# Attention beside a long convolution on one core: when products with V may wait, when the output weights are loaded, and the convolution's allowance

## The chip, the core and the metric

The kernel runs on one core of a Trainium2 chip. The core has a matrix engine (TensorE, PE in the profile; its weight loads are listed as PEld), a vector engine (VectorE, DVE), an engine for functions such as exponentials and sines (ScalarE, ACT), GpSimd (POOL) and SyncE (SP), which here only issues DMAs. Each engine works through its own instructions in order. The metric is device time in microseconds (us), the median of several runs; lower is better.

## What is computed

Two independent parts, concatenated along the last axis. All inputs are fp32.

```
part A (state space convolution), L = 2048, D = 576, N = 128
  dt = exp(log_dt);  A = A_re + i A_im;  B, C complex
  K[d, l] = Re sum_n C[d,n] * exp(dt[d] A[d,n] l) * dt[d] B[d,n]
  y = causal convolution of u with K along l  (reference: FFT of length 2L)
  a = y + u * Dskip

part B (attention, 32 query heads of width 18, one shared key/value head), S = 2048
  q = x wq (32 heads);  k = x wk;  v = x wv
  p = softmax(q k^T / sqrt(18));  o = p v;  b = o wo

result = concat(a, b)          # 2048 x 1152
```

## The kernel before

**The attention** is the spine of the program. Queries are taken in four chunks c of 512 rows, heads in pairs, keys in 16 blocks kb of 128. A *tile* is one pair of heads against one block of keys: `scores` (L466) computes it on PE into one of NS = 3 PSUM buffers "s", `exponentials` (L474) turns it into probabilities "P" on ACT (NP = 8 buffers), and `product` (L765) multiplies two tiles, which is four heads, with V on PE into "ops". So there are 2048 heads-times-blocks in 1024 tiles and 512 products. A *round* handles three tiles: their scores, their exponentials, and the one or two products that come due; `self.step` counts products, so one round is 1.5 steps, and there are 342 rounds. Sixteen steps are a *group* of four heads; `fetch` (L455) then brings the query operands "aug" of later pairs from a DRAM buffer "qd" with SyncE. `gather` copies a finished group out of PSUM ("o") and stores it ("od").

**The side work** of the attention is projections: `qproj` makes the queries of 128 columns at a time ("q", L344) and `queries` stores them to "qd" with GpSimd; `outproj` and `outproj_part` multiply normalised outputs with the output weights "wo_sb" ("op"). The last chunk's remaining output products, and its normalisation, are done after the loop in `finish` ("fin").

**The convolution** works on 12 blocks k of 48 channels. `front(k)` makes the kernel K from small tables of sines, cosines and exponentials: `arguments` and `factors` on DVE and ACT, `tables` ("tab") on DVE, `kgen` ("kg") on PE. Odd blocks prepare the factors of the next even block too (tile "stage") and store them ("fr"). `back(k)` transforms u and K ("hu", "lu", "hk", "lk"), multiplies the spectra on DVE ("us", "ks", "acc", "pt"), and transforms back ("iy"); "outa" is stored at its end. ACT needs another table for sines than for exponentials, so the sines of a block are issued together, as a *burst*: a table load, two or four sines (L1048, L1049), and a table load back before the next exponential of the attention (L474).

**What sets the order.** The instruction order on PE, ACT and DVE is written out when the program is built, by a planner. `Clock` holds estimated times: K.t of PE, K.a of ACT, K.v of DVE, K.s the times at which the three score buffers come free. In each round of `main`, after scores and exponentials, `fill(then)` puts side work and convolution work on PE until the estimated time `then`, each product is placed, and `free()` says when the next scores can begin. A product may stay behind for one round:

```
while behind < r // 2:
    fill(free() - 0.88 * (r // 2 - behind))
    if behind == r // 2 - 1 and K.t + 0.88 > free() + DEFER:
        break
    product(behind)
    behind += 1
```

The side work and the convolution are generators that say at each yield what they need next: "p" a piece of PE work, "v" a piece of DVE work, "w" wait, "b" a burst of sines. A "b" is held until 8 or more pieces of projection work are open (`beside`), or 16 steps have passed. The convolution has a budget: `Conv.go` refuses work when what it has placed on DVE is over 20 us above `step * RATE`, and lets DVE's queue run deeper (up to 1 us) by how far it is below `step * RATE`. `Conv.lags` is true when it is below `step * PACE` and has a piece of PE work next; side work is then passed over, unless a due time is within 8 steps or a projection is half done.

**Loads.** `load_wo` (L326 and L328) writes one element per row block of wo_sb with DVE and then issues five DMAs on SyncE; because of the memset, they wait for DVE to reach it. It is called as the first thing of `main`. `Conv.start` (the transform matrices "dft", L1292, and two blocks of u, L969) stands just ahead of it on SyncE, the first `fetch` of queries just behind.

Of the kernel before, what the change touches and what calls it, by code (L numbers as in the profile page):

```python
# [38 lines left out]
NP = 8  # L39


RATE = 1.79
PACE = 1.72
AHEAD = 0.7
TOTAL = 340.0
LAST = 500
DEFER = 0.5
# [134 lines left out]
class Attention:  # L182
# [521 lines left out]
    def main(self, conv, flag):  # L704
        nc, K = self.nc, self.k
        conv.beside = lambda: self.o_left + self.q_left
        side = self.side_work
        self.load_wo()
        K.t = K.v = K.a = self.o_free = 0.0
        K.fill = 0.0  # L710
        side.ready = 0.0
        for st in conv.streams:
            st.ready = 0.0
        prep = Stream(self.prepare(), K, 99.0)
        pairs = [(c, g, kb, j) for c in range(NCH) for g in range(8) for kb in range(16) for j in range(2)]
        state = dict(credit=0.0, filled=0.0)

        def holder():
            return next((st for st in [side] + conv.streams if st.holds), None)

        def force(done):
            while not done():
                st = holder()
                (side if st is None else st).advance()
                self.fetch(self.group)

        def fill(then):

            t, idle = K.t, 0.0
            more = True  # L730
            while more:
                more = False
                credit = state["credit"] - (K.t - t - idle)
                urgent = self.due < self.step + 8
                late = self.late()
                for st in (prep, side, conv) if urgent else (prep, conv, side):

                    if st is side and side.kind == "p" and not (urgent or side.holds) and conv.lags(self.step):
                        continue
                    spare = credit - 0.3 if st is not side or urgent or late or side.holds else 0.0  # L740
                    wait = then - K.t - (1.2 if st is side and not urgent and not side.holds and self.units > 0.6 * self.step + HEAD else 0.15)
                    if st.go(self.step, max(spare, wait, 0.3 * (st is side and side.holds and conv.lags(self.step) and credit > -1.0)), holder()):
                        more = True
                        break
                else:

                    at = min((x for x in (st.event() for st in [prep, side] + conv.streams) if x > K.t), default=then)
                    if at < then - 0.5:
                        idle += at - K.t
                        K.t = at  # L750
                        more = True
            t += idle
            if K.t > t:
                K.t += 0.03
            state["filled"] += K.t - t
            state["credit"] = max(state["credit"] - (K.t - t), -0.8)

        def product(n):
            nonlocal o_ps
            c, g, kb, _ = pairs[2 * n]  # L760
            if kb == 0:
                fill(self.o_free)
                o_ps = self.ps_o.tile([P, CT], F32, tag="o", name=f"ops{c}_{g}")
            for j in range(4):
                nc.tensor.matmul(o_ps[32 * j:32 * j + 32, :], self.v[:, kb, :], pts[2 * n + j // 2][:, j % 2, :],  # L765
                                 start=(kb == 0), stop=(kb == 15), tile_position=(0, 32 * j))
            K.pe(0.88, done[2 * n + 1] + 0.1, self.o_free if kb == 0 else 0.0)
            read[n] = K.t + 0.2
            state["credit"] -= 0.88
            if kb == 15 and (c, g) != (NCH - 1, 7):  # L770
                self.gather(c, g, o_ps)
                if g == 7:
                    self.todo.append((c, range(5)))
                if c == NCH - 1 and g in LATE:
                    self.todo.append((c, LATE[g]))
        o_ps, pts, done, read, behind = None, {}, {}, {}, 0
        for r in range(0, len(pairs), NS):
            new = range(r, min(r + NS, len(pairs)))
            self.step = new[-1] // 2
            ss = {}  # L780
            for i in new:
                c, g, kb, j = pairs[i]
                if (g, kb, j) == (0, 0, 0):
                    self.od[c] = self.dr.tile([8 * P, CT], F32, tag="od", name=f"od{c}")
                force(lambda: 16 * c + 2 * g + j in self.ready)
                ss[i] = self.scores(i, c, 2 * g + j, kb, 0.335 if i == r else 0.215)
            K.t += 0.22
            for i in new:

                while (i - NP) // 2 >= behind:  # L790
                    product(behind)
                    behind += 1
                c, g, kb, j = pairs[i]
                pts[i] = self.exponentials(i, c, 2 * g + j, kb, *ss[i], read.get((i - NP) // 2, 0.0))
                done[i] = K.a
            s = self.step

            state["credit"] = min(state["credit"] + NS / 2 * (0.88 + min(max((TOTAL - state["filled"]) / max(LAST - s, 20), 0.45), 0.7 if s < 384 else 0.9)), 1.2 + 0.88)

            def free():  # L800

                return max(K.s[(r + NS + j) % NS] - 0.22 * j for j in range(NS))
            while behind < r // 2:
                fill(free() - 0.88 * (r // 2 - behind))

                if behind == r // 2 - 1 and K.t + 0.88 > free() + DEFER:
                    break
                product(behind)
                behind += 1
            fill(free())  # L810
            c, g, kb, j = pairs[new[-1]]
            self.group = (new[-1] + 1) // 32
            self.fetch(self.group)
            nxt = 16 * c + 2 * g + 3
            if kb >= 12 and nxt < 64:
                force(lambda: nxt in self.ready)
        while behind < len(pairs) // 2:
            product(behind)
            behind += 1

        while self.todo or self.busy or holder() or any(m == 0 for _, _, m in self.rest):
            if self.todo or self.busy:
                prep.advance()
            elif holder() or self.outs:
                (holder() or side).advance()
        conv.drain()
        nc.vector.tensor_scalar(flag, self.ubound[0:1, :], LIMIT / (2 * SCALE), None, op0=ALU.is_le)
        self.finish(NCH - 1, self.part, o_ps, self.w4, self.b4)
# [86 lines left out]
class Conv:  # L915
# [100 lines left out]
    def factors(self, k):  # L1016


        nc, V, p1, K = self.nc, self.V, self.pf, self.k
# [5 lines left out]
        if k % 2 == 0 and k > 0:  # L1025
            yield "v", self.kept_ready, False
            f, r = self.kept
        else:
            f, r, m = (p1.tile(shp, F32, tag=t, name=f"{n}{k}") for t, n in (("f", "f"), ("r", "r"), ("sum", "m")))
# [13 lines left out]
            if both:  # L1043
                nc.scalar.activation(m2, m2, AF.Exp)
                K.act(1.25)
            yield "b", K.v + 0.3, False
            for r_, f_ in ((r, f), (r2, f2)) if both else ((r, f),):
                nc.scalar.activation(r_, r_, AF.Sin, scale=-TWO_PI, bias=self.hp)  # L1048
# [229 lines left out]
    def early(self):  # L1278
        nc = self.nc
        nc.scalar.dma_start(self.pos, self.a["pos"])  # L1280
        self.load(0)
        self.n = -1
        self.streams = [Stream(self.front(0), self.k)]

    def begin(self):
# [19 lines left out]
    def go(self, step, credit, lock):  # L1305
        self.turn()
        lag = step * RATE - self.work
        if lag < -20.0:
# [16 lines left out]
    def lags(self, step):  # L1325
        return self.work < step * PACE and any(st.live and st.kind == "p" for st in self.streams)

# [105 lines left out]
```

## Time and profile before

| what | value |
|---|---|
| median of 3 runs (lowest to highest) | 1222.99 us (1221.77 to 1226.05) |
| the profiled execution, and its span | 1222.96 us, 1221.1 us |
| mean clock granted to PE | 0.985 |
| PE, ACT, DVE, POOL busy | 94%, 85%, 80%, 10% |
| bytes moved by DMA, mean rate | 102.15 MB, 84 GB/s |
| exponentials of the attention on ACT | 1024 of 1030 ns, 968.6 us |
| matmul instructions of the products with V, of the scores | 4096 (520.9 us busy), 2048 (366.3 us busy) |

How to read it. The page of the profile lists the busy time of each engine, the chain of work that ended last (each step followed back to what released it), and groups of instructions by line, `out<-in` in the program's names, count and duration. A row in order of time has start, length, engine, line, operation, operands, the count of instructions merged, and in brackets the idle time of the engine ahead of it with what ended it. A row of windows has a stretch of time, its length, each engine's busy time with its instruction count, PE's granted clock (1.00 is full), the mean busy share of the 16 DMA engines, and GB/s. Rows with SPq or ACTq are the queues that issue. An fp32 matmul of the program shows as two instructions, so a product is 8 rows' worth and a score tile 2. "issue" means that nothing visible was late.

### The profile page before, as it was taken

Reading aid. Unit: us, or ns where it says so; the run is one execution under the profiler, and the core shown is the slowest. Engines: PE = TensorE matmul, PEld = TensorE weight load, DVE = VectorE, ACT = ScalarE, POOL = GpSimd, SP = SyncE. Lnnn points to the kernel's source line nnn. Section 1 sums busy time; section 2 is a strip of 40 time slices with the busy share of each in tenths; the row PEclk is TensorE's granted clock in tenths of the full one; section 3 lists DMA queues with packets and bytes.
Section 4 is the critical chain, followed back from the end, with each engine's and each line's share of the span. In section 5 each row is a group of like instructions: output and inputs, shape, how many; then the busy total and the mean of one; then the engine's idle time right before and its main releaser. Section 6 shows DMA issues by size and latency. Waiting matters only on the chain.

```text
span 1221.1 us, 32917 instructions
## 1 busy us (share of the span) xinstructions
PE 1141.8 (94%) x13852; PEld 471.5 (39%) x13852; DVE 973.2 (80%) x1599; ACT 1033.3 (85%) x1091; POOL 118.6 (10%) x210
## 2 busy tenths in 40 slices
PE   5989899999899999989999989999997999989997
PEld 1433333434343444434344334444342434433433
DVE  4757965997997896996997996993975899689684
ACT  2769989878898988998898998888899888899891
POOL 2220401011211000011020000002040000000000
PEclk9989999999999999999999999999998999999999
DMA  7533323124243112132234122114123111211201
GB/s 227 146 131 88 103 81 114 39 60 120 87 143 98 60 35 86 40 126 92 69 103 138 41 69 91 50 56 115 61 75 119 69 51 35 90 45 43 67 28 55
DMA packets 61713, 102.15 MB, mean 84 GB/s; under 512 B 17692, under 2 KB 28570, under 8 KB 61048
## 3 DMA queue, kind: packets, MB, share of 16 engines
q1 hardware_dynamic: 47046, 85.32, 21.4%
q0 software_dynamic: 13824, 14.07, 4.4%
q8 instruction: 111, 1.82, 0.6%
q10 hardware_dynamic: 690, 0.60, 0.2%
q14 instruction: 42, 0.34, 0.1%
HBM read 55.66 MB, written 42.89 MB: 81 GB/s over the span
## 4 chain that ended last, share of the span: by engine, by line
PE 70%; DVE 12%; ACT 10%; issue 4%; DMA 4%; SPq 1%; ACTq 0%; DVEq 0%
PE ops L765 29%; PE s L466 21%; ACT P L474 8%; PE q L344 4%; PE op L179 4%; PE iy L179 3%; PE kg L1130 3%; DVE ks L109 2%; DMA xr<-xT 2%; PE hu L179 1%; DVE acc L109 1%; PE fin L179 1%; DVE tab L109 1%; PE hk L179 1%; DVE pt L109 1%
## 5 line engine op out<-in xcount | busy, mean ns | idle before, releaser
L474 ACT ACTIVATE P<-s 128x1024 f32<-128x1024 f32 x1024 | 968.6, 1030 | 144.5 <-PE s L466 142.3
L765 PE MATMUL ops<-P,v_sb 128*32 128x512 f32 x4096 | 520.9, 602 | 14.0 <-DVE o L113 13.9
L466 PE MATMUL s<-aug,kaug 55*128 55x512 f32 x2048 | 366.3, 445 | 35.0 <-ACT P L474 27.7
L466 PEld LDWEIGHTS s<-aug,kaug 55*128 55x128 f32 x2048 | 170.1, 186 | 348.8 <-ACT P L474 311.9
L765 PEld LDWEIGHTS ops<-P,v_sb 128*32 128x32 f32 x4096 | 114.2, 110 | 163.5 <-issue 118.5
L409 POOL DMA_DIRECT2D qd<-qh x116 | 66.0, 575 | 466.9 <-DVE qh L113 466.8
L344 PE MATMUL q<-x,wq_sb 128*32 128x256 f32 x1360 | 85.3, 385 | 1.1 <-DVE un L121 1.0
L179 PE MATMUL op<-wo_sb,oT 126*32 126x288 f32 (+1 forms) x1040 | 74.1, 409 | 4.0 <-DVE ob L113 2.7
L113 DVE COPY ksb<-kg 128x192 f32<-128x192 f32 x48 | 17.4, 364 | 58.0 <-PE kg L1130 57.7
L109 DVE TENSOR_TENSOR tab<-tab,tt 128x576 f32<-128x576 f32 (+1 forms) x72 | 59.1, 821 | 1.8
L109 DVE TENSOR_TENSOR tab<-r,dif 128x576 f32<-128x576 f32 (+1 forms) x72 | 58.8, 816 | 0.0
L109 DVE TENSOR_TENSOR tab<-sum,r 128x576 f32<-128x576 f32 (+1 forms) x72 | 58.7, 816 | 0.0
L109 DVE TENSOR_TENSOR tab<-tab 128x576 f32<-128x576 f32 (+1 forms) x72 | 58.7, 815 | 0.0
L109 DVE TENSOR_TENSOR tt<-f,sum 128x576 f32<-128x576 f32 (+1 forms) x72 | 58.6, 815 | 0.0
L344 PEld LDWEIGHTS q<-x,wq_sb 128*32 128x32 f32 x1360 | 40.8, 111 | 45.4 <-issue 20.4
L109 DVE TENSOR_TENSOR acc<-acc,pt 128x1728 f32<-128x1728 f32 (+2 forms) x36 | 48.6, 1350 | 0.3
L109 DVE TENSOR_TENSOR pt<-us,ks 128x1728 f32<-128x1728 f32 (+2 forms) x36 | 48.1, 1350 | 0.1
L179 PEld LDWEIGHTS op<-wo_sb,oT 126*32 126x32 f32 (+1 forms) x1040 | 30.4, 109 | 44.3 <-issue 17.6
L109 DVE TENSOR_TENSOR u<-u,iy 128x384 f32<-128x384 f32 x24 | 13.3, 553 | 39.1 <-PE iy L179 39.0
L1130 PEld LDWEIGHTS kg<-tab 128*32 128x32 f32 x2304 | 36.2, 110 | 21.2 <-issue 12.0
L446 POOL DMA_DIRECT2D qd<-sh x19 | 12.0, 633 | 315.2 <-DVE sh L117 311.3
L1130 PE MATMUL kg<-tab 128*32 128x64 f32 x2304 | 41.7, 220 | 0.0
(134 smaller groups left out, 999.3 us busy)
## 6 DMA issues: line engine op xcount, KB each, us to landing
aug<-qd SPq DMA_DIRECT2D x124, 110.0 KB
od<-o SPq DMA_DIRECT2D x31, 256.0 KB
fr<-stage SPq DMA_DIRECT2D x10, 624.0 KB
qd<-qh POOLq DMA_DIRECT2D x24, 216.0 KB, 4.6
u<-u SPq DMA_DIRECT2D x12, 384.0 KB
kd<-ksb SPq DMA_DIRECT2D x12, 384.0 KB
kt<-kd SPq DMA_DIRECT2D x48, 96.0 KB
outa<-u SPq DMA_DIRECT2D x12, 384.0 KB
```

Of the source, the lines that this page charges most:

```text
L109: return self.v.tensor_tensor(out, *a, **k)
L113: return self.v.tensor_copy(out, *a, **k)
L179: nc.tensor.matmul(ps[j:e], w[:, j:e], x, start=start, stop=stop, tile_position=(0, j))
L344: nc.tensor.matmul(ps[o, 256 * f:256 * f + 256], w[:, k, i], xt[:, k, x], start=(k == 0), stop=(k == 4), tile_position=(0, 32 * j))
L409: q.dma_start(qd[h:h + n, row + d:row + d + nd, cs], src[i1:i1 + n * nd, :cs.stop - cs.start].bitcast(F32))
L446: q.dma_start(qd[h0 + n0:h1, 54, :].rearrange("p (a n) -> p a n", a=2), two(sh, h1 - h0 - n0))
L466: nc.tensor.matmul(ps[:, j, :], self.kaug[r, kb * P:(kb + 1) * P], t[r, :], start=True, stop=True)
L474: nc.scalar.activation(pt, ps, AF.Exp, scale=SCALE)
L765: nc.tensor.matmul(o_ps[32 * j:32 * j + 32, :], self.v[:, kb, :], pts[2 * n + j // 2][:, j % 2, :], start=(kb == 0), stop=(kb == 15), tile ...
L1130: nc.tensor.matmul(ps[32 * g:32 * g + 32, d, :], t[:, :32], t[:, 32:], start=(j == 0), stop=(j == 1), tile_position=(0, 32 * g))
```

## The change

Three edits that work on the planner alone. The arithmetic is the same, and only the order of instructions and the place of one load differ.

1. `RATE` goes from 1.79 to 1.83 and `PACE` from 1.72 to 1.76.
2. `load_wo` is not called at the start of `main`, but in the round with r = 96, the 33rd.
3. The convolution has a flag `burst`, set just before it yields "b" in every block but the first. While it is set, the loop over products may leave two products behind instead of one (`off`), does so as soon as placing one would make the next scores late (`much` is 0.0 in place of DEFER, 0.5), and lets `fill` run one product longer. The flag is cleared once ACT's planned time is over 4 us ahead of PE's, as it is when sines have been placed. Without the flag, the loop is as before.

```diff
-RATE = 1.79
-PACE = 1.72
+RATE = 1.83
+PACE = 1.76
...
         side = self.side_work
-        self.load_wo()
         K.t = K.v = K.a = self.o_free = 0.0
...
             s = self.step
+            if r == 96:
+
+                self.load_wo()
...
+            off, much = (2, 0.0) if conv.burst else (1, DEFER)
+            if K.a > K.t + 4.0:
+                conv.burst = False
             while behind < r // 2:
-                fill(free() - 0.88 * (r // 2 - behind))
-
-                if behind == r // 2 - 1 and K.t + 0.88 > free() + DEFER:
+                fill(free() - 0.88 * max(r // 2 - behind - off + 1, 0))
+                if behind >= r // 2 - off and K.t + 0.88 > free() + much:
                     break
                 product(behind)
                 behind += 1
...
                 nc.scalar.activation(m2, m2, AF.Exp)
                 K.act(1.25)
+            self.burst = k > 0
             yield "b", K.v + 0.3, False
...
         self.load(0)
-        self.n = -1
+        self.n, self.burst = -1, False
```

## The prediction

> **What bounds the kernel now.** I read the page first: busy time of the engines, then the chain that ended last. After that I looked for the places where the chain is not TensorE at work, in windows.
>
> ```profile
> span 1221.1 us, 32917 instructions
> PE 1141.8 (94%) x13852; PEld 471.5 (39%) x13852; DVE 973.2 (80%) x1599; ACT 1033.3 (85%) x1091; POOL 118.6 (10%) x210
> PE 70%; DVE 12%; ACT 10%; issue 4%; DMA 4%; SPq 1%; ACTq 0%; DVEq 0%
> ```
>
> TensorE (PE) is busy for 1141.8 of 1221.1 us and carries 70% of the chain. The change removes no arithmetic, so all that can be won is among the 79.3 us in which PE is idle, and the stretches in which its clock is reduced. Two places stand out. The first is near the start, while inputs are loaded (windows: PE, PEld, DVE, ACT and POOL busy, then clock, DMA share, GB/s; then PE's and SyncE's instructions in order, and what SyncE's queue waited for):
>
> ```profile
> 56.00:66.00 10.00, 9.47 (x182) 4.36 (x178) 4.05 (x11) 8.36 (x9) 4.54 (x8) 1.00 0.89 280
> 66.00:72.00 6.00, 2.15 (x6) 0.96 (x6) 5.90 (x11) 2.14 (x3) 1.11 (x2) 0.64 0.81 296
> 72.00:78.00 6.00, 6.00 (x31) 1.68 (x35) 0.27 (x1) 2.07 (x3) 0.00 (x0) 0.51 0.19 64
> ...
> 59.32 0.97 PE L466 MATMUL s<-aug,kaug 55*128 55x512 f32 x6
> 62.74 0.96 PE L466 MATMUL s<-aug,kaug 55*128 55x512 f32 x6
> 67.51 1.13 PE L466 MATMUL s<-aug,kaug 55*128 55x512 f32 x4 [2.04 <-issue]
> 70.54 0.76 PE L466 MATMUL s<-aug,kaug 55*128 55x512 f32 x1 [1.91 <-DMA aug<-qd]
> 71.74 0.79 PE L466 MATMUL s<-aug,kaug 55*128 55x512 f32 x1 [0.43 <-DMA aug<-qd]
> 72.46 3.64 PE L765 MATMUL ops<-P,v_sb 128*32 128x512 f32 x16
> 76.03 1.65 PE L466 MATMUL s<-aug,kaug 55*128 55x512 f32 x6
> ...
> 56.17 4.36 SPq L328 DMA_DIRECT2D wo_sb<-wo  x5
> 61.71 10.33 SPq L455 DMA_DIRECT2D aug<-qd  x10
> SPq L455 <- DMA wo_sb<-wo: 4.5, 4, 1.7
> 63.85 7.84 DMA aug<-qd
> ```
>
> Scores of the second head group wait for queries (aug) that SyncE could only issue from 61.71 us, behind the five loads of the output weights, and that travel while the DMA engines are 0.81 to 0.89 busy. From 66 to 78 us PE also runs at a granted clock of 0.64 and then 0.51. The other place is the sine bursts, in which ScalarE (ACT) makes no exponentials:
>
> ```profile
> L1048 ACT ACTIVATE r<-r,hp_sb x7: 1334/1336/1340, 13.8 to 1075.4; 128x1248 f32<-128x1248 f32 x7
> 132.00:154.00 22.00, 16.80 (x156) 6.36 (x152) 21.69 (x27) 21.13 (x21) 7.64 (x13) 0.90 0.34 103
> 694.00:716.00 22.00, 19.04 (x210) 7.08 (x202) 21.86 (x26) 21.74 (x22) 0.00 (x0) 1.00 0.25 98
> 918.00:945.00 27.00, 19.23 (x144) 5.82 (x136) 15.52 (x26) 24.85 (x25) 0.59 (x1) 0.81 0.29 107
> ...
> 147.78 0.51 PE L466 MATMUL s<-aug,kaug 55*128 55x512 f32 x2 [3.54 <-ACT P L474]
> 704.41 2.15 PE L179 MATMUL op<-wo_sb,oT 126*32 126x288 f32 x32 [1.73 <-DVE ob L113]
> 889.97 1.25 ACT L1044 ACTIVATE stage<-stage 128x1248 f32<-128x1248 f32 x1
> 928.15 1.04 PE L765 MATMUL ops<-P,v_sb 128*32 128x512 f32 x8
> 935.98 2.63 PE L466 MATMUL s<-aug,kaug 55*128 55x512 f32 x6 [6.78 <-ACT P L474]
> 938.53 3.34 PE L765 MATMUL ops<-P,v_sb 128*32 128x512 f32 x16
> 942.41 2.86 ACT L474 ACTIVATE P<-s 128x1024 f32<-128x1024 f32 x3 [1.90 <-PE s L466]
> ```
>
> Of the seven bursts the first lies in setup; six remain in the loop. Only the first and fifth of these leave PE idle for want of ACT (3.54 and 6.78 us); in the fourth, for instance, PE has output products to do and its gap is an eviction's (1.73 us).
>
> **The change part by part.** *The output weights.* The load moves from ahead of the loop to round 33. What moves: one memset on VectorE (DVE), five DMA issues on SyncE, and 4 x 283.5 + 162 KB, 1.30 MB. It goes past the first fetch of queries. An undisturbed round at this place takes 62.74 - 59.32 = 3.42 us; the scores that start at 76.03 should have started two rounds after 62.74, at 69.6. So the stall costs 6.4 us, its slow clock included: that is the upper bound. How much goes? SyncE would issue the queries some 5 us earlier, and at 280 to 296 GB/s the 1.30 MB taken out of their way are 4.4 to 4.6 us. The last query needed, landed at 63.85 + 7.84 = 71.69, would land at about 67.2. The scores ahead of it start at 67.51 after 2.04 us in which nothing visible was late, so that wait may stay, and the clock may still dip after it: a dip of the size seen leaves another 2.5 us: the 16 product instructions at 72.46 hold PE until 76.03, 3.57 us, where 16 at the loop's end (row further down) hold it from 1191.89 to 1193.63, 1.74; and six score instructions take 1.65 for 0.96. Lower bound 6.4 - 2.0 - 2.5 = 1.9 us. I take the transfer's 4.5 us, since this is the wait that the rows name; late next is the 2.04 us.
>
> At the new place the load costs nothing by the rows that follow. Ninety-six score tiles are through at about 152 us (the window of the exponentials alone counts 97 from 31 to 152 us), right after SyncE's next fetch of queries, and the next DMA that SyncE has to issue is a store of one head group:
>
> ```profile
> 31.00:152.00 121.00, 92.23 (x97) 0.95 0.39 116
> 151.56 3.18 SPq L455 DMA_DIRECT2D aug<-qd  x4
> 157.76 0.34 SPq L483 DMA_DIRECT2D od<-o  x1
> 156.00:164.00 8.00, 7.40 (x54) 2.27 (x50) 6.92 (x14) 6.31 (x7) 0.00 (x0) 0.98 0.15 55
> L179 PE MATMUL op<-wo_sb,oT x1040: 402/406/431, 385.5 to 1186.9; 126*32 126x288 f32 x142, 72*32 72x288 f32 x32
> ```
>
> The DMA engines are 0.15 busy in the 8 us behind it, and the weights are first read at 385.5 us. SyncE waits for the memset behind whatever DVE has queued; behind SyncE stands that one store, whose reader comes a block of heads later. The memset is one small instruction. If cover is lacking, a pause like the 2.04 us one could come here: lower end -2.0.
>
> *Two products put off.* Between the request for sines and the round after them, PE may keep two products with V in hand instead of one, and does the scores first when late. A product (8 instructions) is 0.87 us of PE, half of that 1.74. In the first burst one more product in the 3.54 us gap saves 0.87. In the fifth, PE restarts cold: the two products at 938.53 take 3.34 us, 1.67 each, and ACT waits 1.90 for the scores behind them. One product done in the 6.78 us gap instead saves 1.67. In the other four, the gap belongs to an eviction and I count nothing. Sum 2.5 us. Bounds: all six bursts at 0.87, and in the first no dip of the clock (below): 5.2 + 3.2 = 8.4. On the other side, ACT could wait for a probability buffer that a postponed product still reads, one product of 0.87 us: -1 us.
>
> The clock behind that gap, in its own row:
>
> ```profile
> 148.00:156.00 8.00, 7.17 (x32) 2.09 (x34) 6.88 (x7) 7.16 (x8) 0.64 (x2) 0.60 0.81 268
> ```
>
> At 0.60 over 8 us the first burst loses 3.2 us of PE's full rate. The gap with a product in it is 3.54 - 0.87 = 2.67 us. The start showed a clock of 0.64 behind pauses of 2.04 and 1.91 us with little work between, so I keep the dip. [...]
>
> *A higher allowance for the convolution.* RATE caps how far the convolution's DVE work may run ahead of the step; PACE is the share below which the projections (the side work) are held back for it. Both go up by 0.04 a step, 20 us of planned work at the end of 512 steps. The end of the loop shows the convolution late, not early:
>
> ```profile
> L1275 SPq DMA_DIRECT2D outa<-u x12: 338/367/1947, 172.0 to 1198.3; - x12
> 1191.89 2.30 PE L765 MATMUL ops<-P,v_sb 128*32 128x512 f32 x16
> 1193.63 1.86 PE L179 MATMUL iy<-w,dft_sb 128*32 128x192 f32 x32
> 1196.15 1.51 PE L179 MATMUL iy<-w,dft_sb 128*32 128x192 f32 x32 [0.66 <-DVE u L109]
> 1197.47 3.58 PE L179 MATMUL fin<-wo_sb,oT 126*32 126x288 f32 x56
> ```
>
> Its last block leaves at 1198.3, behind the last product. A cap on running ahead does not hold back something that is behind, so RATE only lets DVE's queue run a little deeper; PACE acts, and draws TensorE work of the convolution forward. The two inverse transforms at the end (1193.63 to 1197.47) then fall inside the loop. Their matmuls must be done anyway and PE is nearly full there, so only the 0.66 us pause is sure; if they fit into idle time entirely, 3.8. I take 0.7, the row that is a wait. Below nothing: a projection held back while the convolution's step is not ready leaves PE idle for one wait, 1 us or two.
>
> Sum: 4.5 + 2.5 + 0.7 = 7.7 us. The profiled execution took 1222.96, 1.9 more than its span and level with the median of 1222.99. 1222.96 - 7.7 = 1215.3.
>
> **The rivals.** *The start goes on waiting.* The pause of 2.04 us has no cause that the rows name. If it is not the output weights' doing, it stays while the transform matrices and u are still being loaded, the dip follows, and the start gives 1.9. With the gain of the bursts lost to a reshuffled order, the result is 1222.96 - 1.9 = 1221.1; with a pause at round 33 too, no change at all. For it: the DMA engines are 0.89 busy over 56 to 66 us, of which the output weights are less than half (1.30 of 2.80 MB).
>
> *The fifth burst finds work.* Its arguments' exponentials ended at 891.2, but the sines came only when PE's gap began, near 929 us, with no projections at hand; then PE stood 6.78 us and ran at 0.81 of the clock over 27 us (5.1 us). If PACE, holding projections back, leaves some for it, it would look like the fourth: 6.78 - 1.73 + 5.1 = 10.2 us, less the 1.7 already counted, 8.5 better: 1206.8. For it: projections come later. Against: a burst that is fed now may lose its work by the same shift (1215.3 + 10.2 = 1225.5, no change).
>
> [...]
>
> *Slower: projections come in lumps.* Held back whenever the convolution is behind, a query projection gets done only when due, all at once. One lump is in the trace:
>
> ```profile
> 519.80 4.52 PE L344 MATMUL q<-x,wq_sb 128*32 128x256 f32 x80
> ```
>
> Inside a burst that is free. In plain rounds ACT has three tiles of 0.95 in hand, so it starves 4.52 - 2.85 = 1.7 us per lump, and PE pays it later when ACT is the slower. Seven such lumps (11.9 us) outweigh the 7.7 by more than 0.3%; with all 12 or so units of the last three chunks, 1215.3 + 20.4 = 1235.7. From eight lumps on, say 1229. Against: a projection with a nearing due time goes ahead of the convolution already.
>
> **How the numbers follow.** About 0.3% (3.7 us) can be told from no change here: 1219.3 to 1226.7. Chances: the forecast 0.38, the clock rule 0.10, the fifth burst fed 0.22, no change by a start still waiting or a burst that loses its work 0.16, slower by lumps 0.14. Faster 0.70, same 0.16, slower 0.14. The likeliest case's own range is 1211 to 1219. The range for 8 in 10 takes in the fed fifth burst with the deeper end of the start (1206.8 - 1.9 = 1204.9) and no change: 1204 to 1227.
>
> **What would show it.** Right: the queries issued by about 57 us, no wait for them near 70, PE's clock above 0.8 in 66 to 78 us; three products within or right before the sines of the first burst; the last block of the convolution stored before the last product. Wrong: a wait for another DMA at the same place; ACT idle in plain rounds behind long runs of q; a burst with 6 us of idle PE at a new place.

## The result, and the profile after

The changed kernel takes 1213.59 us (median of 6 runs, 1211.18 to 1217.32) against 1222.24 us for the one before (6 runs): ratio 0.9929, 95% interval 0.9915 to 0.9942, so 8.7 us faster (7.1 to 10.4). The forecast was 1215.3, in a range of 1204 to 1227. The number came out; of the terms behind it, one was right, one came to nothing by itself, and one was far too small.

The page of the changed kernel: span and instructions, busy time, and the engines' shares of the chain.

```profile
span 1211.8 us, 32941 instructions
PE 1139.7 (94%) x13852; PEld 467.8 (39%) x13852; DVE 978.1 (81%) x1611; ACT 1033.2 (85%) x1091; POOL 119.7 (10%) x210
PE 69%; DVE 16%; ACT 8%; issue 4%; DMA 2%; SPq 1%; DVEq 0%; ACTq 0%
```

PE's busy time is the same to 2 us, its idle time went from 79.3 to 72.1 us, and its mean granted clock from 0.985 to 0.993. The start, in the windows and rows of before:

```profile
56.00:66.00 10.00, 10.00 (x184) 4.12 (x175) 6.50 (x16) 7.69 (x9) 5.03 (x9) 1.00 0.90 305
66.00:72.00 6.00, 5.52 (x60) 2.21 (x58) 5.93 (x9) 5.79 (x8) 0.61 (x1) 1.00 0.38 124
...
67.20 0.50 PE L466 MATMUL s<-aug,kaug 55*128 55x512 f32 x2 [0.41 <-ACT P L474]
...
56.41 11.35 SPq L455 DMA_DIRECT2D aug<-qd  x10
151.64 2.05 SPq L328 DMA_DIRECT2D wo_sb<-wo  x5
```

The queries go out at 56.41, where they went at 61.71; the wait for them is gone, the pause of 2.04 us too, and the clock is 1.00. The output weights follow at 151.64, and nothing waits for them. Now the first and the fifth sine burst and the end (PE in order of time, the convolution's stores, and the output products that are left):

```profile
133.59 4.52 PE L344 MATMUL q<-x,wq_sb 128*32 128x256 f32 x80
139.75 1.51 PE L179 MATMUL iy<-w,dft_sb 128*32 128x192 f32 x32 [1.63 <-DVE ql L109]
...
873.63 4.52 PE L344 MATMUL q<-x,wq_sb 128*32 128x256 f32 x80
881.20 2.79 PE L179 MATMUL iy<-w,dft_sb 128*32 128x192 f32 x32 [3.05 <-DVE ql L109]
...
1191.67 1.90 PE L764 MATMUL ops<-P,v_sb 128*32 128x512 f32 x16
1193.39 2.61 PE L179 MATMUL fin<-wo_sb,oT 126*32 126x288 f32 x40
L1281 SPq DMA_DIRECT2D outa<-u x12: 338/358/1250, 144.1 to 1158.3; - x12
L179 PE MATMUL fin<-wo_sb,oT x80: 402/406/430, 1193.4 to 1201.8; 126*32 126x288 f32 x80
```

Both bursts have a whole projection in them. Behind it PE stands 1.63 and 3.05 us, waiting for VectorE; before, it stood 3.54 and 6.78 us, waiting for ACT. The last product is over at 1193.39, against 1193.63 before: the loop itself is no shorter. What is shorter is what follows it, 18.4 us in place of 27.5 (span less that time). The convolution is stored at 1158.3, so no inverse transforms are left, and 80 instead of 176 instructions of output products remain. So the loop did that work and is no longer for it. What it won at the start and at the bursts is where the time for it can have come from; this one profile does not show it, and the runs below take it apart.

### The profile page after: what moved, and what is told of

The parts are those of the page before. It is cut to its first block, busy times and chain, and to the rows that moved or that the text cites. A ratio compares the mean times of both kernels' runs of the same rounds, so it can differ in the third digit from the quotient of the medians.

```text
span 1211.8 us, 32941 instructions
## 1 busy us (share of the span) xinstructions
PE 1139.7 (94%) x13852; PEld 467.8 (39%) x13852; DVE 978.1 (81%) x1611; ACT 1033.2 (85%) x1091; POOL 119.7 (10%) x210
## 4 chain that ended last, share of the span: by engine, by line
PE 69%; DVE 16%; ACT 8%; issue 4%; DMA 2%; SPq 1%; DVEq 0%; ACTq 0%
PE ops L764 28%; PE s L466 20%; ACT P L474 7%; PE op L179 4%; PE q L344 4%; PE kg L1136 3%; PE iy L179 3%; DVE ks L109 2%; DVE tab L109 2%; DVE acc L109 2%; DMA xr<-xT 2%; PE hu L179 1%; PE hk L179 1%; DVE pt L109 1%; PE lu L179 1%
## 5 line engine op out<-in xcount | busy, mean ns | idle before, releaser
L179 PE MATMUL op<-wo_sb,oT 126*32 126x288 f32 (+1 forms) x1136 | 82.1, 410 | 5.6 <-DVE ob L113 5.3
L179 PE MATMUL iy<-w,dft_sb 128*32 128x192 f32 x768 | 39.3, 337 | 4.7 <-DVE ql L109 4.7
```

The lines of the kernel that those rows point to most:

```text
L179: nc.tensor.matmul(ps[j:e], w[:, j:e], x, start=start, stop=stop, tile_position=(0, j))
```

## The experiments

Every time is the median, and every ratio is to the kernel before, run on the same chip. "Loop" is the end of the last product in the profiled execution, "after it" is the rest of the span.

| kernel | median us | ratio (95%) | loop | after it |
|---|---|---|---|---|
| before | 1222.2 to 1224.4 | | 1193.6 | 27.5 |
| changed | 1213.59 | 0.9929 (0.9915 to 0.9942) | 1193.4 | 18.4 |
| load alone, round 33 | 1218.12 | 0.9957 (0.9941 to 0.9972) | 1188.9 | 27.4 |
| load alone, round 12 | 1217.71 | 0.9956 (0.9941 to 0.9970) | 1190.8 | 27.2 |
| two products alone | 1224.62 | 1.0008 (0.9994 to 1.0022) | 1197.0 | 25.4 |
| PACE alone | 1215.37 | 0.9939 (0.9923 to 0.9955) | 1192.8 | 19.8 |
| RATE alone | 1217.48 | 0.9945 (0.9930 to 0.9961) | 1200.0 | 18.0 |
| changed, load back | 1216.17 | 0.9935 (0.9923 to 0.9948) | 1196.9 | 18.6 |
| changed, PACE back | 1212.98 | 0.9913 (0.9900 to 0.9926) | 1194.9 | 18.8 |
| changed, RATE back | 1214.93 | 0.9931 (0.9919 to 0.9943) | 1193.6 | 19.5 |
| changed, no burst flag | 1223.52 | 0.9995 (0.9977 to 1.0012) | 1207.5 | 17.8 |
| the same, ql by SyncE | 1226.99 | 1.0028 (1.0011 to 1.0045) | 1211.0 | 16.8 |
| patience 28 | 1242.89 | 1.0163 (1.0144 to 1.0183) | 1189.1 | 50.4 |
| load and PACE | 1208.95 | 0.9886 (0.9863 to 0.9908) | 1186.5 | 19.4 |

### One part at a time

**The load alone.**

```diff
-        self.load_wo()          # ahead of the loop
+            if r == 96:
+                self.load_wo()
```

> The kernel before with the load of the output weights alone moved to round 33; the planned order of TensorE, ScalarE and VectorE stays as it was. Theory 1 (the start is worth its whole stall, and a lead won at the start lasts to the end): 6.4 us faster, about 1216, wait for aug near 70 us gone and clock 1.00 in 66 to 78 us. Theory 2 (a lead at the start is given back, because the changed kernel ends its loop only 0.5 us earlier than before): within 2 us of before, 1220 to 1222.

It is 5.2 us faster (3.4 to 7.2), in an order that is the same on PE, ACT and DVE. The loop ends 4.7 us earlier and the rest is as before, so a lead won at the start lasts in the main, and theory 2 falls. In the two profiled executions the lead is 7.0 us up to the fourth burst (its table load back comes at 699.51 in place of 706.47) and 4.8 at the fifth (928.78 in place of 933.61). Between them lies a stretch in which the clock is 0.92 (694 to 716 us) and was 1.00 before. In windows:

```profile
56.00:66.00 10.00, 10.00 (x178) 4.29 (x170) 3.02 (x7) 8.35 (x10) 5.05 (x9) 1.00 0.81 269
66.00:72.00 6.00, 5.88 (x76) 2.65 (x76) 5.90 (x14) 5.77 (x7) 0.61 (x1) 1.00 0.34 114
```

PE is full in 66 to 72 us, and the clock is whole.

**The load moved only past the first fetches** (r == 33).

> The kernel before with the load of the output weights moved only past the first ten fetches of queries on SyncE (round 12 in place of round 33). If the stall came from what travels or is issued ahead of the queries: as with round 33, 1217 to 1219. If the DMA engines' total load in 56 to 76 us is what counts (the pause of 2.04 us, the slow clock): at most half the gain, 1220 to 1222.

5.4 us, as with round 33. The windows of this kernel:

```profile
66.00:72.00 6.00, 5.90 (x102) 2.74 (x104) 4.15 (x12) 5.82 (x7) 1.55 (x3) 1.00 0.54 149
72.00:78.00 6.00, 5.96 (x80) 2.82 (x82) 4.60 (x8) 5.74 (x7) 0.00 (x0) 1.00 0.64 215
```

The DMA engines carry the same bytes a little later (0.64 busy in 72 to 78 us, where it was 0.13 with round 33), and PE does not notice. What counts is what stands ahead of the queries; round 12 is late enough, and round 33 was not needed.

**The two products alone** (the flag and the loop over products; the rest as before).

> The kernel before with the two postponed products alone. If a postponed product fills ScalarE-bound gaps as I summed it: 2.5 us faster, about 1219.7, with a product inside the first and the fifth sine burst and the fifth still unfed (its gap near 6 us). If the reshuffled order decides: anywhere from 1214 to 1228, according to whether the fifth burst finds projections.

No gain: 1.0 us slower (0.7 faster to 2.7 slower). Its first and fifth burst, and what ACT waited for over the whole execution:

```profile
146.41 0.50 PE L466 MATMUL s<-aug,kaug 55*128 55x512 f32 x2 [3.10 <-ACT P L474]
929.13 1.04 PE L765 MATMUL ops<-P,v_sb 128*32 128x512 f32 x8
936.96 2.63 PE L466 MATMUL s<-aug,kaug 55*128 55x512 f32 x6 [6.79 <-ACT P L474]
939.52 3.64 PE L765 MATMUL ops<-P,v_sb 128*32 128x512 f32 x16
ACT P L474 <- PE ops L765: 5.8, 7, 1.6
```

The gap of the first burst went from 3.54 to 3.10, that of the fifth stayed at 6.79 with one product ahead of it, as before. The postponed product was not put into the gap. And ACT now waits seven times, 5.8 us in all, for a product to release a probability buffer; before, the profile has no such wait. The changed kernel has it too, four times and 5.3 us in all:

```profile
ACT P L474 <- PE ops L764: 5.3, 4, 2.7
```

**PACE alone, RATE alone.**

```diff
-PACE = 1.72          # the one kernel
+PACE = 1.76
-RATE = 1.79          # the other
+RATE = 1.83
```

> The kernel before with PACE 1.76 alone. Theory 1 (the tail and the fed fifth burst come from PACE): last block of the convolution stored before the last product, fifth burst with a projection in it, after the loop 11 to 15 us in place of 27, total about 1214 with the stall at the start still there (clock 0.64 in 66 to 72 us). Theory 2 (PACE only moves the same TensorE work from the tail into the loop): tail shorter, loop longer by as much, 1221 to 1223.

> The kernel before with RATE 1.83 alone. The convolution is behind its share all along, so the cap never holds it; only VectorE's queue may run up to 0.5 us deeper in the middle. By the prediction: nothing, 1222 plus or minus 2. If it is outside 1219 to 1226, a reshuffled order alone is worth more than the terms I summed, which then says how far any single plan can be explained.

PACE alone gives 7.5 us (5.5 to 9.4), and RATE alone 6.7 (4.8 to 8.6): my statement that RATE does nothing is wrong. For each, the window around the fifth burst, the last product, what follows it, and the stores of the convolution; PACE first.

```profile
876.00:900.00 24.00, 20.23 (x246) 8.93 (x238) 22.95 (x32) 22.04 (x22) 9.19 (x17) 0.93 0.49 145
1191.11 1.90 PE L765 MATMUL ops<-P,v_sb 128*32 128x512 f32 x16
1192.83 3.10 PE L179 MATMUL fin<-wo_sb,oT 126*32 126x288 f32 x48
L1275 SPq DMA_DIRECT2D outa<-u x12: 337/356/1317, 150.1 to 1170.5; - x12
```

```profile
884.00:908.00 24.00, 20.66 (x270) 9.52 (x274) 22.64 (x39) 20.07 (x20) 10.86 (x20) 0.93 0.54 162
1198.26 1.90 PE L765 MATMUL ops<-P,v_sb 128*32 128x512 f32 x16
1199.98 2.61 PE L179 MATMUL fin<-wo_sb,oT 126*32 126x288 f32 x40
L1275 SPq DMA_DIRECT2D outa<-u x12: 338/360/546, 172.6 to 1164.9; - x12
```

Either way the fifth burst is fed (20.2 and 20.7 us of PE in 24; before, 19.2 in 27) and the convolution is over 22 and 35 us ahead of the loop's end. The part after the loop is 7.7 and 9.5 us shorter. With PACE, the loop takes in this work for nothing. With RATE, it pays part of it back. This profiled execution of RATE's took 1219.74, at the upper end of its runs.

The shorter part after the loop comes with every kernel of the table that has the new PACE or RATE (16.8 to 19.8 us) and with none that has neither (25.4 or more). The loop's length goes by no such rule (1186.5 to 1211.0 us). RATE's result lies outside 1219 to 1226, and for that case the expectation had said that a reshuffled order alone is worth more than the terms that I summed. That stands: how much of these two gains is the earlier end of the convolution, and how much a luckier order, no run here separates.

### One part taken back

The changed kernel with one edit undone.

> The changed kernel with the load of the output weights back ahead of the loop; the planned order stays that of the changed kernel. If the load's place is worth the same in any plan (5.2 us with it alone): 1213.6 + 5.2 = 1218.8, with the wait for aug and the slow clock back near 70 us. If the plan of the changed kernel covers the stall: within 2 us of 1213.6.

The ratios 0.9935 and 0.9929 do not tell the two apart; the spans differ by 3.7 us. In this order of instructions the queries were a smaller loss to begin with: in 66 to 72 us PE is 3.10 us busy at a clock of 1.00, where before it was 2.15 at 0.64. In the 6 us after that the slow clock does come back, at 0.72 where it was 0.51.

```profile
66.00:72.00 6.00, 3.10 (x22) 1.03 (x18) 5.90 (x10) 4.43 (x6) 1.11 (x2) 1.00 0.79 288
72.00:78.00 6.00, 6.00 (x56) 2.45 (x48) 2.38 (x4) 3.28 (x4) 0.00 (x0) 0.72 0.11 36
```

> The changed kernel with PACE back at 1.72. If RATE and PACE do the same thing (each alone has fed the fifth burst and ended the convolution inside the loop): within 2 us of 1213.6, fifth burst still fed. If PACE is what carries the tail: up to 1220 and the last block again near the end of the loop.

> The changed kernel with RATE back at 1.79. By the prediction RATE does nothing: 1213.6 plus or minus 2. If its 6.7 us alone add to PACE's: near 1220.

Either can go without a loss (0.9913 and 0.9931 beside 0.9929): PACE and RATE both lead to a convolution that is not late (18.8 and 19.5 us after the loop), and in this company their gains do not add.

> The changed kernel without the flag for sine bursts. By my prediction 2.5 us slower than the changed kernel, 1216. By the run with the two postponed products alone (no gain, ratio 1.0008): the same as the changed kernel or faster, 1211 to 1214; in this case the edit named first in the change is worth nothing.

This was the surprise: without the flag, which alone gives nothing, the whole gain is gone. The part after the loop is short as in the changed kernel (17.8 us), and the loop is 14.1 us longer (in a profiled execution of 1227.09, above its median). Its largest wait stands behind the fifth burst (DVE, then GpSimd's issues of the stores, PE, ACT, in order of time):

```profile
900.08 0.42 DVE L113 CAST qh<-q 128x256 fp32r<-128x256 f32 x1
905.22 0.42 DVE L109 TENSOR_TENSOR ql<-q,qh 128x256 fp32r<-128x256 f32 x1 [4.72 <-DMA qd<-ql]
...
894.86 1.64 POOL L409 DMA_DIRECT2D qd<-ql  x3
894.27 1.69 SPq L1064 DMA_DIRECT2D fr<-stage  x2
...
906.48 0.50 PE L179 MATMUL up<-sel_sb,aw 128*32 128x8 f32 x24 [4.43 <-DVE aw L117]
906.82 3.62 PE L764 MATMUL ops<-P,v_sb 128*32 128x512 f32 x16
...
911.25 8.36 ACT L474 ACTIVATE P<-s 128x1024 f32<-128x1024 f32 x9 [7.01 <-PE s L466]
```

Two query projections came close together. The second writes the single buffer ql, whose last contents GpSimd had sent off at 894.86, after six stores of qh and just behind 1.25 MB of factors on SyncE. DVE stood for 4.72 us, PE behind it for 4.43 and then ran at half rate (3.62 us for 16 instructions that take 1.9 elsewhere), ACT for 7.01. To test that, the stores of ql go out by SyncE, with the same order on PE, ACT and DVE:

```diff
-                        q.dma_start(qd[h:h + n, row + d:...
+                        (nc.sync if src is ql else q).dma_start(qd[h:h + n, row + d:...
```

> The changed kernel without the burst flag (1223.5), with the stores of the low query parts (qd<-ql) issued by SyncE in place of GpSimd; the orders of TensorE, ScalarE and VectorE are the same to the instruction. Theory: that kernel loses its gain because two query projections follow each other within 12 us, and VectorE's second write of ql waits 4.72 us for the store of the first, which GpSimd issued late and which travelled beside 1.25 MB of factors; TensorE then idles 4.43 us and ScalarE 7.01. SyncE is free from 888.5 to 894.3, so the store leaves 2 to 3 us earlier and ahead of the factors: the wait falls below 1 us, and the time to about 1217.5. Rival (the loss is spread over the reshuffled order, and this wait is covered): 1222 to 1225.

As a whole this missed: it is 3 to 4 us slower than the kernel without the flag (the two intervals just touch). SyncE's queue is not free at the start, and there ql waits for its own turn (DVE and windows of this kernel):

```profile
64.92 0.69 DVE L109 TENSOR_TENSOR ql<-q,qh 128x512 fp32r<-128x512 f32 x1 [6.53 <-DMA qd<-ql]
56.00:66.00 10.00, 3.62 (x54) 1.67 (x50) 1.77 (x3) 4.68 (x5) 3.32 (x6) 0.92 0.78 245
```

At the place in question it did what was expected in direction. The table load of the fifth burst is at 881.63 without and 891.66 with this edit, 10.0 us later; that of the sixth is at 1049.07 and 1052.49, only 3.4 later. Between the two, in the same order of instructions, 6.6 us were won, a smaller dip of the clock included (0.86 over 912 to 924 us, in place of 0.72 over 902 to 914); DVE there waits 2.31 us for a store of qh, in place of 4.72 for ql:

```profile
912.36 0.42 DVE L113 CAST qh<-q 128x256 fp32r<-128x256 f32 x1 [2.31 <-DMA qd<-qh]
```

So the wait, with the slow clock behind it, costs most of what it seemed to, about half of the 14 us. The trace shows one more place, the clock behind the fourth burst (the kernel without the flag first, then the changed kernel):

```profile
710.00:720.00 10.00, 9.72 (x50) 2.92 (x50) 9.90 (x13) 7.87 (x10) 0.00 (x0) 0.68 0.31 128
700.00:710.00 10.00, 9.92 (x98) 3.75 (x98) 9.81 (x14) 8.33 (x10) 0.00 (x0) 1.00 0.47 185
```

Over the whole execution PE is busy 8.6 us longer for the same 13852 instructions (1148.3 and 1139.7 us) and idle 4.9 us longer, and its mean clock is 0.982 in place of 0.993. So PE at a slower rate makes up much of the loss; what starts each slow stretch is not settled.

### What a late convolution costs

To feed the fifth burst without moving the convolution forward, a burst may be held for 28 steps:

```diff
-                if self.beside() >= 8 or step > st.asked + 16 or self.n < 0:
+                if self.beside() >= 8 or step > st.asked + 28 or self.n < 0:
```

> The kernel before with a burst of sines held up to 28 steps for projection work in place of 16; only the fifth burst has waited its full time, and it now comes when the output products of the third chunk are open. Theory (an unfed fifth burst costs 8.5 to 10 us): the loop ends 8 us earlier, no gap of 6 us; the convolution is later by some 25 us, so up to 6 us of it come back after the loop: 1215 to 1220. Rival (the gain of RATE alone and PACE alone is the convolution's earlier end, not the fed burst): no gain, 1222 to 1230.

```profile
1187.40 1.90 PE L765 MATMUL ops<-P,v_sb 128*32 128x512 f32 x16
1213.24 2.79 PE L179 MATMUL iy<-w,dft_sb 128*32 128x192 f32 x32 [21.75 <-DVE w L109]
L1275 SPq DMA_DIRECT2D outa<-u x12: 338/360/1532, 168.9 to 1218.9; - x12
```

The burst was fed, and the loop ended at 1189.1, 4.5 us earlier than before, where I had expected 8. Of these, 2.1 were there before the edit acts (the table load back of the fourth burst is at 704.39, before at 706.47). The convolution's work moved as well, so this run gives no clean price for a fed fifth burst; by the end of the loop it is well under the 8.5 that I had put on it. But the convolution was held up with the sines, which came 21 us later than before (948.9 for 927.5), and PE then stood 21.75 us after the loop while DVE finished the last block alone. I had expected 6. Before the change, this cliff was 1 us away: DVE was done with the last block's "w" at 1192.5, and PE came to it at 1193.6.

```profile
1190.55 1.96 DVE L109 TENSOR_TENSOR w<-sv 128x384 f32<-128x384 f32 x4
```

### A version that beats both

The load at round 33 and PACE 1.76; RATE and the products as before.

> The kernel before with the load moved to round 33 and PACE 1.76, without the postponed products and with RATE 1.79. If single gains add: 1223.4 - 5.2 - 7.5 = 1210.7, faster than the changed kernel. By the runs that leave one part out (the load is worth 2.6 us in the changed plan): 1212 to 1215. If every plan with PACE and without postponed products meets crowded projections: about 1220.

```profile
1184.80 1.90 PE L764 MATMUL ops<-P,v_sb 128*32 128x512 f32 x16
1186.52 3.10 PE L179 MATMUL fin<-wo_sb,oT 126*32 126x288 f32 x48
L1276 SPq DMA_DIRECT2D outa<-u x12: 337/357/1591, 145.3 to 1164.2; - x12
```

1208.95 us, ratio 0.9886: here the two single gains add, to 14 us (11.3 to 16.8). It is some 5 us faster than the changed kernel (0.9886 with at most 0.9908, beside 0.9929 with at least 0.9915). Adding RATE to it is the kernel without the flag, at 1223.52; adding the flag as well is the change.

## Why the prediction was right or wrong

**The load, 4.5 us: right.** Alone it gave 5.2, through the wait that was named, and the place in the queue is the cause (round 12 does as well). The term lies inside the measured interval (3.4 to 7.2). The pause of 2.04 us with no visible cause, which I left in, went with the load: four of the six kernels that load first have it (2.04 to 2.19 us; the other two wait 2.33 and 2.81 us at this place for something that the trace names), and none of the eight that load later. What it waits for stays open. Inside the changed order the load's new place is worth between 0 and 4 us. I had taken the stall as the same in any order, and 6.4 us as its upper bound; the lead in the profiled execution was 7.0 before the slow stretch near 700 us.

**Two products, 2.5 us: wrong in the mechanism.** I put the extra product into ACT's gap. The planner puts it behind: the gaps stayed (3.10 and 6.79 us), and the bound that I had set at one product of 0.87 us, ACT waiting for a probability buffer, came to 5.8 us in seven waits, and to 5.3 in the changed kernel. Alone the edit gives nothing. In the change it decides 8 us (0.9995 beside 0.9929). As far as the traces show, that comes from the order that it happens to lead to: with it, the crowded projections at 900 us do not arise.

**RATE and PACE, 0.7 us: the size was far off, and RATE was misread.** I counted the one wait at the end (0.66 us) and took the rest of the work after the loop as due anyway. Measured alone it is 7.5 and 6.7 us, since the 27.5 us after the loop shrink to 18 to 20, while the loop takes in the work, with PACE at no cost and with RATE at part of it. That the 27.5 us were due anyway is the step that failed in this term. A cap does not hold back what is late, but RATE also sets how deep DVE's queue may run, and I waved this off as "a little deeper". That RATE acts by the depth is read from the code; no run separates it from the cap, or from the luck of the order.

**The rivals.** The fed fifth burst came true (chance 0.22), but its time of 1206.8 did not: the burst won less by the end of the loop than I had priced, and the other terms did not simply add to it. The lumps of projections (0.14) do exist: without the flag, two of them close together cost about half of what is lost, by a buffer that is still being stored and not by PE's own time as I had it. The clock rule (0.10), by which PE would run at a full clock behind the first burst's gap, is shown by no run: where the products alone were changed, the gap was 3.10 us and the clock behind it 0.57 (148 to 156 us; 0.60 before), and in the changed kernel a projection fills the gap (4.52 us from 133.59).

**The signs listed.** Queries issued by 57 us (56.41), a whole clock in 66 to 78 us, and the last block stored ahead of the last product all came. Three products inside the sines of the first burst did not.

So 7.7 predicted and 8.7 measured agree in part by accident: a term too large by 2.5, one too small by 6, and a loss of about 5 against the best combination that I did not foresee.

## What to carry to other kernels

In a queue that one engine issues in order, look at what stands ahead of the first thing that is waited for: 1.3 MB that nobody needed for 330 us cost 5 us. Work that runs beside a bottleneck must end before it, with room: sines held up by 21 us came back as a wait of 21.75 us. In an order written by a planner, parts that gain alone may add (the load and PACE, 14 us) or undo each other (RATE on top of these two took all of it back), so smaller sets are to be run as well, and not only the full one.

## What the hardware showed that was not expected

The clock dipped behind gaps of under 2 us. In the kernel without the flag, PE was idle for 1.89 us, and the next 16 product instructions took 3.59 us, near twice their 1.9, at a granted clock of 0.60 from 958 to 962 us:

```profile
958.01 0.86 PE L179 MATMUL hu<-u,dft_sb 128*32 128x192 f32 x16 [1.89 <-DVE scu L109]
958.66 3.59 PE L764 MATMUL ops<-P,v_sb 128*32 128x512 f32 x16
```

In the changed kernel a projection after 1.73 us of idle time took 6.21 us for 80 instructions (first the stretch that ends in this pause, with a whole clock):

```profile
502.00:505.40 3.40, 1.67 (x32) 0.69 (x27) 3.37 (x6) 3.40 (x4) 0.00 (x0) 1.00 0.03 2
505.26 6.21 PE L344 MATMUL q<-x,wq_sb 128*32 128x256 f32 x80 [1.73 <-DVE ob L113]
```

With the load put back, the same instructions after the same gap took 4.53:

```profile
510.05 4.53 PE L344 MATMUL q<-x,wq_sb 128*32 128x256 f32 x80 [1.73 <-DVE ob L113]
```

Same order, same pause, once slow (a granted clock of 0.76 from 505 to 512 us) and once not (1.00 from 510 to 517): so the length of the gap alone does not decide it. What else does, no run here shows.
